# A planned order of issue for the first 14 FFN steps, batch 1's attention and the weight conversion

## The chip, the cores and the metric

The kernel runs on one core of a Trainium2 chip. The metric is the device time of one execution in microseconds (us). A core has five engines, each with its own instruction queue: TensorE (PE in the profile, PEld for its weight loads), VectorE (DVE), ScalarE (ACT), GpSimd (POOL) and SyncE (SP, which here issues the loads and stores). Engines wait for each other through semaphores. Matmuls write to eight PSUM banks of 2 KB per partition; all else lies in SBUF.

## What is computed

```python
# attention, for each of 8 batches and 8 heads (576 tokens, 64 wide)
q_d, k_d, v_d = (a.reshape(B, H, 144, 4, D).mean(axis=3) for a in (q, k, v))
out_up = np.repeat(softmax(scale * q_d @ k_d.T) @ v_d, 4, axis=2)      # coarse part
mask = np.abs(pos[:, None] - pos[None, :]) < 4
out_local = softmax(np.where(mask, scale * q @ k.T, -1e9)) @ v         # band part
x = (out_up + out_local) as 4608 tokens x 512
# FFN, 512 -> 2048 -> 512
h = x @ w_in
g = s * np.maximum(h, 0.0) ** 2 + b
return g @ w_out
```

The weights arrive as float64 and are read as pairs of 32-bit words.

## The kernel before

**FFN.** The 4608 tokens are 18 tiles of 256 (index t), the 2048 hidden columns 8 parts of 256 (index p). A step is a pair (t, p). `gemm1` (lines 551 to 570) makes one part of h in one PSUM bank: 24 matmuls over 256 columns, three for each product, since x and the weights are split into a high and a low float32r part (hi times hi, hi times lo, lo times hi; lines 556 to 558). ScalarE then applies ReLU and the square and rounds to `gh`, VectorE makes the rest `gl` (lines 566 to 569). `gemm2` (lines 586 to 616) multiplies by w_out with 12 matmuls over 512 columns and accumulates over p in two banks. It runs two steps behind `gemm1`. The order of steps (lines 653 to 656) is: 14 steps with p from 0 to 6 and t = 0, 1 in turn; t = 2 with p from 0 to 6 (steps 14 to 20); p = 7 for t = 0, 1, 2; then t from 3 on with all p. TensorE therefore meets each new part of the weights as it is converted.

**Conversion.** `convert` (lines 214 to 234) turns a staged block of float64 words into the high and low float32r parts: a scaled copy on ScalarE (line 226), four operations on VectorE (227 to 230), a rounding copy on ScalarE (231), and a subtraction on VectorE (234). `split_w(p)` does this for w_in's and w_out's part p. The scratch is a pair of tiles `pv` for p = 0, 1, 7 and the tiles `xl2` and `os` for the others. `CHUNK` sets the columns per operation, `CONVERT_AT` the step after which each part is converted, `BEHIND` how far its priority is lowered.

**Attention.** A unit is one batch and two heads. `down` (lines 268 to 342) is the coarse part: sums of four tokens on VectorE and GpSimd, scores `sa`, softmax, transposes `tp` and `tr`, and the product `up`. `first_unit` (lines 344 to 440) runs `down` for a unit of batches 0 to 2 and, between its stages, the band part with small matmuls: two score tiles `sl`, softmax, a transpose to blocks `bd`, two products `ol`. `up` is copied to `ups` (line 421), and line 434 adds `ol` and the repeated `ups` into x. Batches 3 to 7 use `two_pairs`, which does the band part on GpSimd and VectorE (`local_unit`) and the coarse part with `down_unit`, whose ScalarE copy (line 448) writes the repeated `up` into x.

Each unit takes eight PSUM tiles one after the other: sa, sl, sl, tp, tr, up, ol, ol. Batch 0 takes them from a ring of seven banks (line 638), batch 1 from banks 5 and 6 in turn, batch 2 from bank 5 and then from 2, 3 and 5 (line 662). FFN uses bank 4, bank 7 for t = 1 in the first 14 steps, and banks 0 to 3 for its sums. A bank is taken again once its last reader is done.

Batch 0's units 1 to 3 borrow tiles of the FFN (`make_room`, lines 89 to 102): the places of converted weights, and for the exponentials `pl` of units 2 and 3 parts of the tiles `os` and `xl2` (line 97).

**Order.** A scheduler in the framework fixes each engine's order of instructions when the kernel is built, by priorities and its own estimate of times; on the chip each engine follows that order. The program steers it by the order of the calls and by `high_priority(offset)`. Batch 0 has an offset of 400 (line 643). From step 0 on, `advance` (lines 680 to 686) runs the attention of later batches as a generator, so many yields per step that batch b is ready when its tokens are due (`need`, `free`, `NY`, lines 629, 658 to 678); batch 1's yields have an offset of 300. Lines 691 to 707 are the loop over steps.

`split_x(t)` (lines 529 to 546) splits a token tile into its high and low parts; tile 2 needs tokens of batches 0 and 1 and uses the tiles `os` and `xl2`. `add_rows` (lines 572 to 579) sums rows of w_out for the bias term, one part p per step, from step 13 on.

Of the kernel before, what the change touches and what calls it, by code (L numbers as in the profile page):

```python
# [11 lines left out]
F32 = mybir.dt.float32  # L12
# [50 lines left out]
def attention_ffn_kernel(ctx, tc, qk, vw_in, vr_in, vdm, qkn, vn, w_in, w_out, s_in, b_in, out):  # L63
# [127 lines left out]

    wi, wo, wst = {}, {}, {}
# [4 lines left out]
    def load_w(p):  # L197

        parts = (("i", src_i[:, :, 512 * p : 512 * p + 512]), ("o", src_o[:, 2 * p : 2 * p + 2]))
        for op, src in parts:  # L200
# [13 lines left out]
    def convert(st, hi, lo, op, p):  # L214


        n = hi.shape[1]
        top, low = st[:, :, 1], st[:, :, 0]
        if p in (0, 1, 7):
            f = two.tile([P, n], F32, tag="pv", name="es")  # L220
        else:
            f = one.tile([P, n], F32, tag="xl2" if op == "i" else "os", name="es")
        w = f.bitcast(I32)


        nc.scalar.mul(f, top.bitcast(F32), 2.0 ** -112)
        nc.vector.tensor_scalar(f, f, W_MAX, -W_MAX, ALU.min, ALU.max)
        nc.vector.tensor_scalar(w, w, 3, 0x7FFFFFF8, ALU.logical_shift_left, ALU.bitwise_and)
        nc.vector.scalar_tensor_tensor(w, low, 29, w, ALU.logical_shift_right, ALU.bitwise_or)
        nc.vector.scalar_tensor_tensor(w, top, -0x80000000, w, ALU.bitwise_and, ALU.bitwise_or)  # L230
        nc.scalar.copy(hi, f)
        for i in range(0, n, 512):
            js = slice(i, min(i + 512, n))
            nc.vector.tensor_tensor(lo[:, js], f[:, js], hi.bitcast(F32)[:, js], ALU.subtract)

    def split_w(p):
        with tc.high_priority(offset=-BEHIND.get(p, 0)):
            split_parts(p)

    def split_parts(p):  # L240
        wi[p] = one.tile([P, 2, NK, 256], F32R, tag=f"wi{p}", name="wi")
        wo[p] = one.tile([P, 2, 2, DM], F32R, tag=f"wo{p}", name="wo")
        for op, w in (("i", wi[p]), ("o", wo[p])):
            fl = w.rearrange("p s k f -> p s (k f)")
            if p < len(STAGE):
                st = wst.pop((p, op))
                for j in range(0, 1024, CHUNK[p]):
                    js = slice(j, j + CHUNK[p])
                    convert(st[:, js], fl[:, 0, js], fl[:, 1, js], op, p)
            else:  # L250
                for i in range(4):
                    cs = slice(256 * i, 256 * i + 256)
                    convert(load_quarter(p, op, i), fl[:, 0, cs], fl[:, 1, cs], op, p)
# [14 lines left out]
    def down(b, hp, banks, tmp, dg):  # L268
# [6 lines left out]
        kd = tmp([P, SD], "kd")  # L275
        nc.vector.tensor_reduce(
            qd, qt[:, 0:S].rearrange("p (s j) -> p s j", j=FAC), AX.X, ALU.add)
        nc.vector.tensor_reduce(
            kd, kt[:, 3 : 3 + S].rearrange("p (s j) -> p s j", j=FAC), AX.X, ALU.add)
        for h in range(2):  # L280
# [18 lines left out]
        dsm = tmp([P, NQ], "dsm")[0:n]  # L299
        sa = banks([n, NQ, SD], "sa")  # L300
        with first(b):
            for i in range(NQ):
                nc.tensor.matmul(sa[:, i], qc[:, i], kd, start=True, stop=True)  # L303
        nc.vector.tensor_reduce(dmx[:, 0], sa, AX.X, ALU.max, negate=True)
# [465 lines left out]
```

## Time and profile before

| | |
|---|---|
| time, median of 3 runs | 974.49 us (971.71 to 974.57) |
| the profiled execution's own time | 972.49 us |
| its span, first to last instruction | 970.7 us |
| PE busy | 938.7 us, 97% of the span |
| DVE, ACT, POOL busy | 637.7, 475.0, 418.0 us |
| mean granted TensorE clock | 1.00 |

The page gives the busy time of each engine, its share in 40 equal slices, the chain of waits that ended last, the costliest groups of instructions and the DMA issues. A row of a group reads: line, engine, operation, output <- inputs, partitions x elements, count | busy us, mean ns of one | idle time of the engine just before them and what ended it. A row of the timeline reads: start, duration, engine, line, and in brackets the idle time before it and its releaser. Matmuls are pipelined, so their durations overlap; the distance between two starts is the pace. The tiles that batch 0's units 1 to 3 borrow are all named `flat`.

### The profile page before, as it was taken

To read this page: it belongs to the slowest core of one execution; us is meant where nothing else is said; L and a number is where in the kernel's file an instruction comes from. 1 tells how busy PE (TensorE), PEld (TensorE's weight loads), DVE (VectorE), ACT (ScalarE), POOL (GpSimd) and SP (SyncE) were. 2 spreads that over 40 slices of the span, in tenths; PEclk is the share of its full clock that TensorE was granted. 3 is DMA by queue.
4 is the path that set the end of the run, shared out by engine and by line. 5 is a ranking of instruction groups with operands and counts; after the bars stand their busy time and mean duration, and the time that the engine had idled before them with its cause. 6 is when DMAs were issued, how large, how long until landed. Compare 5 with 4: busy or idle time off the path is not lost.

```text
span 970.7 us, 18541 instructions
## 1 busy us (share of the span) xinstructions
PE 938.7 (97%) x7316; PEld 843.4 (87%) x7316; DVE 637.7 (66%) x1175; ACT 475.0 (49%) x1141; POOL 418.0 (43%) x455
## 2 busy tenths in 40 slices
PE   5769999999999999999999999999999999999998
PEld 4559988888999999998888899989899999998987
DVE  5999996864567878787787878787878521211121
ACT  5878775553754453545363545453635433333231
POOL 9421011101066686776868786867676200000000
PEclk9999999999999999999999999999999999999999
DMA  9736512112243232323241424242412000000000
GB/s 316 261 121 210 172 60 78 49 42 73 101 134 113 77 110 72 102 70 133 67 136 66 135 68 131 72 134 69 136 55 76 1 22 1 23 1 22 1 23 22
DMA packets 32103, 86.26 MB, mean 89 GB/s; under 512 B 3344, under 2 KB 7952, under 8 KB 32016
## 3 DMA queue, kind: packets, MB, share of 16 engines
q1 hardware_dynamic: 32016, 85.08, 26.6%
q8 instruction: 57, 0.93, 0.4%
q14 instruction: 30, 0.25, 0.1%
HBM read 75.63 MB, written 9.44 MB: 88 GB/s over the span
## 4 chain that ended last, share of the span: by engine, by line
PE 74%; DVE 9%; DMA 8%; POOL 5%; ACT 2%; issue 2%; SPq 0%; DVEq 0%; ACTq 0%; POOLq 0%
PE ph L556 11%; PE ph L557 11%; PE ph L558 11%; PE po L603 11%; PE po L601 11%; PE po L602 11%; DMA tqk<-in_qk_dram 3%; POOL pr L466 3%; POOL acc L488 3%; DMA wst<-in_moe_w_out_dram 2%; PE sa L303 2%; DVE bias L579 1%; PE up L339 1%; PE ol L431 1%; DMA lqk<-in_qkn_dram 1%
## 5 line engine op out<-in xcount | busy, mean ns | idle before, releaser
L556 PE MATMUL ph<-xh,wi 128*128 128x256 f32 x1152 | 325.4, 283 | 3.7 <-ACT xh L542 2.5
L557 PE MATMUL ph<-xl,wi 128*128 128x256 f32 x1152 | 323.9, 281 | 0.0
L558 PE MATMUL ph<-xh,wi 128*128 128x256 f32 x1152 | 323.6, 281 | 0.0
L466 POOL TENSOR_TENSOR pr<-lqk 128x576 f32<-128x576 f32 x140 | 201.2, 1461 | 73.2 <-DMA lqk<-in_qkn_dram 29.2
L556 PEld LDWEIGHTS ph<-xh,wi 128*128 128x128 f32 x1152 | 217.5, 189 | 11.2 <-ACT xh L542 2.8
L557 PEld LDWEIGHTS ph<-xl,wi 128*128 128x128 f32 x1152 | 217.4, 189 | 5.4 <-issue 0.2
L558 PEld LDWEIGHTS ph<-xh,wi 128*128 128x128 f32 x1152 | 217.6, 189 | 0.3
L566 ACT ACTIVATE ph<-ph 128x512 f32<-128x512 f32 x144 | 83.8, 582 | 229.0 <-PE ph L558 223.2
L601 PE MATMUL po<-wo,gh 128*128 128x512 f32 x456 | 180.7, 396 | 0.0
L602 PE MATMUL po<-wo,gh 128*128 128x512 f32 x456 | 180.5, 396 | 0.0
L603 PE MATMUL po<-wo,gl 128*128 128x512 f32 x456 | 177.9, 397 | 0.0
L569 DVE TENSOR_TENSOR gl<-ph,gh 128x512 fp32r<-128x512 f32 x114 | 77.8, 683 | 115.8 <-ACT gh L568 115.5
L488 POOL TENSOR_TENSOR acc<-acc,pv 128x576 f32<-128x576 f32 x80 | 114.4, 1430 | 57.1 <-DVE acc L488 29.5
L468 DVE TENSOR_REDUCE st<-pr 128x9 f32<-128x576 f32 x140 | 105.9, 757 | 37.7 <-POOL pr L466 35.4
L292 POOL TENSOR_TENSOR dq<-vq 64x64 f32<-64x64 f32 x58 | 22.8, 393 | 197.4 <-PE up L337 195.3
L603 PEld LDWEIGHTS po<-wo,gl 128*128 128x128 f32 x456 | 85.7, 188 | 17.6 <-issue 0.2
L487 DVE TENSOR_TENSOR pv<-lv,st 128x576 f32<-128x576 f32 x120 | 87.5, 747 | 18.8 <-POOL acc L488 18.4
L601 PEld LDWEIGHTS po<-wo,gh 128*128 128x128 f32 x456 | 85.7, 188 | 15.9 <-ACT gh L568 0.6
L602 PEld LDWEIGHTS po<-wo,gh 128*128 128x128 f32 x456 | 85.7, 188 | 15.8
L568 ACT CAST gh<-ph 128x512 fp32r<-128x512 f32 x114 | 66.9, 587 | 64.3 <-PE po L602 62.4
L567 ACT ACTIVATE ph<-ph 128x512 f32<-128x512 f32 x144 | 83.7, 582 | 3.2
L602 PE MATMUL po<-wo,gb 128*128 128x512 f32 x120 | 47.1, 392 | 0.0
(149 smaller groups left out, 1239.3 us busy)
## 6 DMA issues: line engine op xcount, KB each, us to landing
tqk<-in_qk_dram SPq DMA_DIRECT2D x30, 584.0 KB, 4.1
lqk<-in_qkn_dram SPq DMA_DIRECT2D x20, 768.0 KB, 4.2
lv<-in_vn_dram SPq DMA_DIRECT2D x20, 480.0 KB, 3.4
out_dram<-os SPq DMA_DIRECT2D x17, 512.0 KB, 3.1
wst<-in_moe_w_in_dram SPq DMA_DIRECT2D x7, 1024.0 KB, 6.5
wst<-in_moe_w_out_dram SPq DMA_DIRECT2D x7, 1024.0 KB, 5.3
tvd<-in_vdm_dram SPq DMA_DIRECT2D x29, 160.0 KB, 2.9
tvr<-in_vr_dram SPq DMA_DIRECT2D x29, 128.0 KB, 3.1
```

Source lines behind the costliest of these rows:

```text
L466: nc.gpsimd.tensor_tensor(pr, lqk[:, 0:CH], lqk[:, CH + o : 2 * CH + o], ALU.mult)
L468: nc.vector.tensor_reduce(ls[:, :, o], pr, AX.X, ALU.add)
L487: nc.vector.tensor_tensor(pv, lv[:, o : o + CH], w, ALU.mult)
L488: (nc.vector if o % 3 == 1 else nc.gpsimd).tensor_tensor(acc[:, :, h], acc[:, :, h], pv, ALU.add)
L556: nc.tensor.matmul(ph[:, j], wi[p][:, 0, k, f], xh[:, k], start=(k == 0), stop=False)
L557: nc.tensor.matmul(ph[:, j], wi[p][:, 0, k, f], xl[:, k], start=False, stop=False)
L558: nc.tensor.matmul(ph[:, j], wi[p][:, 1, k, f], xh[:, k], start=False, stop=(k == NK - 1))
L566: nc.scalar.activation(ph, ph, AF.Relu)
L567: nc.scalar.activation(ph, ph, AF.Square)
L601: nc.tensor.matmul(po[m], gh[:, j, ms], wo[p][:, 0, j], start=first, stop=False)
L602: nc.tensor.matmul(po[m], gh[:, j, ms], wo[p][:, 1, j], start=False, stop=False)
L603: nc.tensor.matmul(po[m], gl[:, j, ms], wo[p][:, 0, j], start=False, stop=last)
```

## The change

1. The functions of attention, conversion, `split_x`, `gemm1` and `gemm2` become generators. Before each piece of work they yield a record of it: engine, estimated us, whether it takes or gives back a PSUM bank, and a condition.
2. `plan()` runs the first 14 FFN steps, batch 1's four units and the conversion of p = 1 to 6 as parallel streams through a small simulation with these estimates, and issues each piece when the simulation begins it. Among pieces that could begin on an engine within `WAIT` of the first, the lowest rank goes first. All of this stands in `tc.manual_schedule(engines=ENGINES)`: TensorE, VectorE and ScalarE follow the order of issue there. SyncE and GpSimd don't stand in that set.
3. The conversion in the plan has four lanes, each with a scratch of 512 columns in `xl2` or `os`, for p = 1 too. For w_out of p = 1 to 6 the subtraction on VectorE becomes a negated copy on ScalarE and a DMA issued from GpSimd that adds f to it. For a p = 7 chunk, and for p = 0, the work is as before.
4. `first_unit` is parted into `down_unit` and `band_unit`. `up` is copied by ScalarE, repeated, into x (as in `down_unit` before), and the band part adds `ol` to x; `ups` goes. Within the plan, `tr` is taken after `tp` is copied.
5. Batch 0 takes its banks from two couples of four, 0 to 3 for even and 4 to 7 for odd units; the two parts of a unit follow each other in the order AABBBAABABB, which is the order that `first_unit` had.
6. In batch 2 the coarse part of the next unit runs between the stages of the band part of this one.
7. Behind the plan, split_x(2) and the conversion of p = 7 follow; before, they came with step 13 and step 11. `add_rows` starts one step later. `NY` counts 11 yields per unit.

```diff
-CONVERT_AT = (1, 2, 4, 6, 7, 8, 11)
-CHUNK = (512, 512, 512, 1024, 1024, 512, 1024)
-BEHIND = {1: 400, 2: 100, 4: 100, 5: 400}
+CHUNK = 512
+ADDED, X_AT, LOAD, LAT, BUSY, LANES, WAIT = 5.0, 12.0, 9.0, 0.2, 1.7, 4, 0.25
+PACE, PAIR = 6.6, 22.0
+TURNS = "AABBBAABABB"
+BY_TRANSFER = [(op, p) for op in "o" for p in range(1, 7)]
...
+        yield step("A", 0.62)
+        nc.scalar.mul(f, top.bitcast(F32), 2.0 ** -112)
+        yield step("V", 0.36)
+        nc.vector.tensor_scalar(f, f, W_MAX, -W_MAX, ALU.min, ALU.max)
...
+        if adds:
+            yield step("A", 0.62)
+            nc.scalar.mul(lo, f, -1.0)
+            nc.gpsimd.dma_start(lo, f, accum_op=ALU.add)
+            yield step("D", ADDED)
         else:
-            f = one.tile([P, n], F32, tag="xl2" if op == "i" else "os", name="es")
...
+            yield step("V", 0.64)
+            nc.vector.tensor_tensor(lo, f, hi.bitcast(F32), ALU.subtract)
...
+    def down_unit(b, hp, banks):
+        x = new_x(b)
+        up = yield from down(b, hp, banks, spot(b, hp), diag[0 if b else hp])
+        yield step("A", 0.66, give=True)
+        nc.scalar.copy(
+            x[:, hp].rearrange("p (s j) -> p s j", j=FAC),
+            up.unsqueeze(2).to_broadcast([P, SD, FAC]))
+        yield
...
-            nc.vector.tensor_tensor(
-                x[:, hp, f * (S // 2) : (f + 1) * (S // 2)].rearrange("p (s j) -> p s j", j=FAC),
-                ol.rearrange("p (s j) -> p s j", j=FAC),
-                ups[:, n * f : n * f + n].unsqueeze(2).to_broadcast([P, n, FAC]), ALU.add)
+            yield step("V", 0.45, give=True)
+            xf = x[:, hp, f * (S // 2) : (f + 1) * (S // 2)]
+            nc.vector.tensor_tensor(xf, ol, xf, ALU.add)
...
+    def plan():
+        free = {"P": 0.0, "A": 0.0, "V": 0.0, "D": 0.0}
+        held = {5: 0.0, 6: 0.0}
+        streams = []
+        todo = [(p, op, i) for p in range(1, HF) for op in "io" for i in range(1024 // CHUNK)]
...
+                slow = 1.0 if at > X_AT or engine == "P" else BUSY
+                self.ready = at + us * slow + LAT
+                if engine != "D":
+                    free[engine] = at + us * slow
...
+                down_stream[0].rank = X_AT + PAIR * (hp + 1) - 8.0
+                yield from down_unit(1, hp, lambda *a: down_stream[0].bank(*a))
...
+                band_stream[0].rank = X_AT + PAIR * (hp + 1)
+                yield from band_unit(1, hp, lambda *a: band_stream[0].bank(*a))
...
+                me[0].rank = X_AT + PACE * (2 * p + 2 * (op == "o")) - 6.0
+                yield from split_chunk(p, op, i, f)
...
+        while streams:
+            begins = [(s.begin(), s) for s in streams]
+            begins = [(at, s) for at, s in begins if at is not None]
+            at, s = min(begins, key=lambda b: b[0])
+            engine = s.want[0]
+            at, s = min(((a, s) for a, s in begins if s.want[0] == engine and a <= at + WAIT),
+                        key=lambda b: (b[1].rank, b[0]))
+            s.emit(at)
...
-    bk = banks(0, 1, 2, 3, 5, 6, 7)
+    couples = banks(0, 1, 2, 3), banks(4, 5, 6, 7)
...
-            for _ in first_unit(0, hp, bk):
+            bk = couples[hp % 2]
+            for _ in in_turn("AABBBAABABB", A=coarse(down_unit(0, hp, bk)), B=coarse(band_unit(0, hp, bk))):
...
+    with tc.manual_schedule(engines=ENGINES):
+        plan()
+    done = NY[1]
+    for _ in split_x(2):
+        pass
+    split_w(NFP - 1)
     for st, (t, p) in enumerate(order):
-        gemm1(t, p)
...
+        if st < 2 * HF:
+            continue
```

The FFN stream has the rank infinity, so it yields to the others where both could begin; the evictions have the rank -1 and come first. X_AT is the time on the plan's own clock at which x of batch 0 is expected; operations of ScalarE and VectorE that begin earlier are taken to last BUSY times as long. Loads of weights for p + 2 are issued when a part's last chunk is done, loads of batch 1's units from the coarse stream.

More of the change, by code (lines that the diff above doesn't have):

```diff
@@ L189, in clear, with step, run, coarse @@
         diag[i] = (take(da, 0, [P, 2 * NG, P]), *blocks(da, n, vm))
+    def step(engine, us, take=False, give=False, when=None):
+        return engine, us, take, give, when
+    def run(gn):
+        for _ in gn:
+            pass
+    def coarse(gn):
+        for said in gn:
+            if said is None:
+                yield
     wi, wo, wst = {}, {}, {}
@@ L212, in load_quarter, with convert @@
         return st
[L214 to L217 removed]
+    def convert(st, hi, lo, f, adds=False):
         top, low = st[:, :, 1], st[:, :, 0]
[L219 to L234 removed]
@@ L236, in split_w @@
-    def split_w(p):
[L237 to L253, printed above, removed]
+        w = f.bitcast(I32)
@@ L513, in two_pairs @@
             load_pair(b, 2 * g + u)
-        dn = chain(*(down_unit(b, 2 * g + u, banks) for u in range(2)))
+        dn = chain(*(coarse(down_unit(b, 2 * g + u, banks)) for u in range(2)))
         lo = local_unit(b, g, banks)
```

303 lines of the change are left out of this document (239 added, 64 removed).

## The prediction

> **What bounds the kernel now.** I read the page's first part, busy time by engine, and then the same in five stretches that I cut at the first dense FFN matmul (69.24), at the first matmul of step 14 (159.25) and at step 28 (250.50).
>
> ```profile
> PE 938.7 (97%) x7316; PEld 843.4 (87%) x7316; DVE 637.7 (66%) x1175; ACT 475.0 (49%) x1141; POOL 418.0 (43%) x455
> ```
>
> ```profile
> core 0: us, PE busy (x) PEld busy (x) DVE busy (x) ACT busy (x) POOL busy (x), PEclk, DMA share, GB/s
> 0.00:25.00 25.00, 14.16 (x281) 11.22 (x281) 13.01 (x29) 12.15 (x39) 22.68 (x64) 1.00 0.96 315
> 25.00:69.24 44.24, 30.67 (x421) 25.01 (x421) 43.01 (x98) 36.44 (x96) 15.10 (x18) 1.00 0.56 189
> 69.24:159.25 90.01, 90.01 (x902) 80.76 (x900) 81.73 (x156) 66.57 (x143) 10.66 (x18) 1.00 0.43 142
> 159.25:250.50 91.25, 89.49 (x861) 77.25 (x860) 59.04 (x113) 44.34 (x110) 7.67 (x12) 1.00 0.19 62
> 250.50:970.70 720.20, 714.37 (x4857) 649.15 (x4855) 440.91 (x782) 315.52 (x755) 361.88 (x344) 1.00 0.22 72
> ```
>
> From 69.24 on TensorE is busy in 90.01 of 90.01, 89.49 of 91.25 and 714.37 of 720.20 us: 7.6 us of idle time in 901. It is the bound there, and the change takes no matmul away, so nothing is to be had in that part. The head is another matter: 69.24 us pass before the dense matmuls, TensorE idles 10.84 + 13.57 = 24.4 us in them, and in the second stretch the full engine is VectorE, 43.01 of 44.24. So I ask two things: how much earlier the first step can start, and how much longer the 14 steps then take. What is left of the difference runs through to the end.
>
> The TensorE rows around the first step show how its queue behaves.
>
> ```profile
> 64.57 0.58 PE L556 MATMUL ph<-xh,wi 128*128 128x256 f32 x1 [2.50 <-ACT xh L542]
> 67.06 2.24 PE L431 MATMUL ol<-db,tvw 128*64 128x96 f32 x24 [1.91 <-ACT db L414]
> 69.24 0.58 PE L557 MATMUL ph<-xl,wi 128*128 128x256 f32 x1
> ...
> 69.83 0.41 PE L556 MATMUL ph<-xh,wi 128*128 128x256 f32 x1
> 70.04 0.41 PE L557 MATMUL ph<-xl,wi 128*128 128x256 f32 x1
> ...
> 73.07 0.28 PE L558 MATMUL ph<-xh,wi 128*128 128x256 f32 x1
> 73.19 0.28 PE L556 MATMUL ph<-xh,wi 128*128 128x256 f32 x1
> ```
>
> Step 0 begins at 64.57 with one matmul. Its second stands behind 24 matmuls of batch 1's first unit (db, tvw), which idle 1.91 us for a copy of ScalarE. So issue order alone cost 2 to 4 us. The pitch falls from 0.21 to 0.12 us between 70 and 73: the first 3 us run at half pace, a cost that the change moves and doesn't remove.
>
> The VectorE rows of batch 0: the maximum of the coarse scores of units 0, 1 and 3, the last sum into x of units 1 (44.46) and 3 (65.35), and the first split of x.
>
> ```profile
> 9.04 0.60 DVE L304 TENSOR_REDUCE dmx<-sa 96x3 f32<-96x432 f32 x1 [1.91 <-PE sa L303]
> ...
> 18.56 0.59 DVE L304 TENSOR_REDUCE flat<-sa 96x3 f32<-96x432 f32 x1
> ...
> 34.17 0.59 DVE L304 TENSOR_REDUCE flat<-sa 96x3 f32<-96x432 f32 x1
> ...
> 44.46 0.45 DVE L434 TENSOR_TENSOR x<-ol,flat 128x288 f32<-128x288 f32 x1
> ...
> 65.35 0.44 DVE L434 TENSOR_TENSOR x<-ol,flat 128x288 f32<-128x288 f32 x1
> 65.72 1.21 DVE L543 TENSOR_TENSOR xl<-x,xh 128x1024 fp32r<-128x1024 f32 x1
> ```
>
> From unit 0 to unit 3 the maxima lie (34.17 - 9.04)/3 = 8.4 us apart. Unit 1 needs 26.4 us from its maximum to x, unit 3 even 31.6.
>
> **Part 1: the head.** Two things change in it.
>
> First, the banks. In the ring of seven, unit 1's second local score tile stands on the bank of unit 0's transposed weights, its next ones on unit 0's up and ol, and so on along the chain. With couples, units 0 and 1 share no bank; unit 2 waits only for unit 0, unit 3 only for unit 1.
>
> Second, what VectorE does beside it. These groups are from the stretch 25.00 to 69.24.
>
> ```profile
> L229 DVE SCALAR_TENSOR_TENSOR es<-wst,es 128x512 int32<-128x512 int32 x10 | 6.8, 675 | 0.0
> L230 DVE SCALAR_TENSOR_TENSOR es<-wst,es 128x512 int32<-128x512 int32 x10 | 6.6, 675 | 0.0
> L227 DVE TENSOR_SCALAR es<-es 128x512 f32<-128x512 f32 x10 | 4.8, 493 | 0.4 <-ACT es L226 0.4
> L228 DVE TENSOR_SCALAR es<-es 128x512 int32<-128x512 int32 x10 | 4.4, 440 | 0.0
> ...
> L234 DVE TENSOR_TENSOR wo<-es,wo 128x512 fp32r<-128x512 f32 x4 | 2.7, 668 | 0.0
> ```
>
> Ten chunks of 512 columns go through: four of p=0, which steps 0 and 1 want, and six of p=1 and 2, which they don't. A chunk costs (6.8 + 6.6 + 4.8 + 4.4)/10 + 0.67 = 2.93 us. The six are 17.6 us of the 43.01. In the changed kernel they can't stand there: their scratch is now xl2 and os, which hold the exponentials of batch 0's units 2 and 3 (make_room, line 97) until those are transposed; before, p=1 used pv, which was free. So about 43.0 - 17.6 = 25.4 us of VectorE work remains (with some of batch 1's first unit in it), and by VectorE alone step 0 could start at 25 + 25.4 = 50. By the chain: two units at a time, each in unit 1's 26.4 us, which is with today's crowding. Units 0 and 1 go from 10 to 36; unit 3's scores start when unit 1 has given back their bank, somewhere halfway, at 23, and end at 49; the split of x, 1.2 us, gives 50 too. As in-order waits come on top, I take 55. The ends are 49 (everything fits) and 65 (only the 4 us of issue order go).
>
> **Part 2: the 14 steps.** They now hold all four units of batch 1, and so one more than the 90.01 us did, (1,0). Its price comes from the pitch:
>
> ```profile
> 104.06 0.39 PE L601 MATMUL po<-wo,gh 128*128 128x512 f32 x1
> 104.29 0.39 PE L602 MATMUL po<-wo,gh 128*128 128x512 f32 x1
> ...
> L557 PE MATMUL ph<-xl,wi 128*128 128x256 f32 x112 | 32.5, 290 | 0.0
> ...
> L602 PE MATMUL po<-wo,gh 128*128 128x512 f32 x48 | 19.3, 402 | 0.0
> ```
>
> In the stretch stand 3 x 112 matmuls at 0.12 and 3 x 48 at 0.23 us, 40 + 33 = 73 us, plus 1.5 for the slow start. The remaining 15.5 us are three units: 5.2 each. Dense, the 14 steps take 90.0 + 5.2 = 95.2.
>
> Do the others keep up? VectorE did 13.0 + 43.0 + 81.7 = 137.7 us up to step 14. Off it go 12 subtractions of 0.67 (8 us) and the quarters of p=7 that now follow the plan (up to 10, from five of the 256-wide chunks). So about 120 to 130 us stand against 55 + 95 = 150, less the 12 us that VectorE idles in the first 25. It fits, at 90%. ScalarE did 12.2 + 36.4 + 66.6 = 115.2. On it come 12 negated copies and the wider copies of up, 8 of them up to step 14:
>
> ```profile
> L448 ACT COPY x<-up 128x576 f32<-128x576 f32 x20 | 12.8, 642 | 11.0 <-PE up L339 10.7
> ```
>
> That is at most 8 x 0.64 = 5 us, and 12 x 0.64 = 8 us by the same row: 128 us. Both engines have room, but with three engines at 85 to 100%, each issuing in a fixed order, waits like the 1.91 us above will occur. Thirty-two bank takes of batch 1 and 14 evictions stand in the order; I take 3 us in all, from none to 12. So the 14 steps take 98.
>
> **The adds by transfer.** No row shows one. The nearest is a 256 KB load:
>
> ```profile
> wst<-in_moe_w_in_dram SPq DMA_DIRECT2D x4, 256.0 KB, 2.8
> ```
>
> An add reads two streams and writes one, so 2.8 to 5.6 us; the planner allows 5.0, and wo of p is wanted two steps after wi, 11 us. I take no cost. If one lands later than planned, ScalarE's next chunk on that scratch waits and the evictions stand behind it; 0.6 us x 12 = 7 us is the dear end. The other end is below nothing, since a lane freed before plan only helps. The two single-source operations L227 and L228 are the place to look for trouble: together 0.93 us per chunk, so an issue on GpSimd that had to wait one pair out would come to 3.7, still inside 5.0. The Trainium skill, page "SBUF — State Buffer", section "SBUF: two separate sides", speaks against this edit: a transfer issued from GpSimd starves for descriptors while VectorE runs such an operation, and one of about 620 ns took about 3100. By its added 2.5 us a transfer would take 5.3 and cost 12 x 0.3 = 4 us at most; no run so far shows it.
>
> GpSimd's queue holds batch 1's sums over v behind these issues; it is busy 10.66 of 90.01 us, which covers them. SyncE's loads are the same ones, at 0.43 of the DMA engines. Batch 2's new order uses the same banks, in a stretch where VectorE is 65% busy: nothing. Step 14 needs all of batch 1 for split_x(2), which now comes behind the whole plan: 0 to 3 us, I take 0.5.
>
> **Sum.** 55 + 98 + 0.5 + (91.25 + 720.20) = 965, and 1.8 around the span (the execution took 972.49 for a span of 970.7): 967. The profiled execution lies 2.0 below the median of 974.49. About 0.3%, 2.9 us, is what can be told from no change: faster is below 971.6, slower above 977.4.
>
> **Rivals.** *The head stays long*: the last unit is held by GpSimd and the loads, as the first stretch's 22.68 of 25 us and DMA share of 0.96 suggest, and only issue order is gained: 65 + 98 + 812 + 2 = 977. Against it: from 25 on both are half idle. *The fixed order stalls* (the other sign): batch 1's pieces stand in TensorE's queue at estimated times, and every estimate that is short holds the FFN behind it, as at 64.57. Twelve to fifteen us more in the 14 steps: 979 to 982. It decides once waits exceed 69.24 - 55 - 5.2 = 9 us, five like the 1.91 seen. For it: TensorE then has no idle time to hide them. Against it: the estimates follow the rows (0.64 for L229's 0.675). *The adds starve*, ScalarE's queue with them: 4 to 7 us, about 973, later still if they are beyond 6 us each. *All fits*: 49 + 95.2 + 811.5 + 1.8 = 957.5.
>
> **Chances.** The forecast 0.50, the long head 0.15, the stalls 0.17, the starved adds 0.04, all fits 0.14. Faster: 0.44 + 0.02 + 0.02 + 0 + 0.14 = 0.62. Same: 0.06 + 0.07 + 0.04 + 0.01 = 0.18. Slower: 0 + 0.06 + 0.11 + 0.03 = 0.20. The forecast's own range is 958 to 973; to leave out no more than 2 in 10, I reach to 956 and 979.
>
> **What would show it.** The first dense matmul of FFN near 55, not 65; the maxima of units 0 and 1 within 4 us; no chunk of p=1 before unit 2's transpose; step 14 at about 153; TensorE's idle time over 3 us in the 14 steps if the order stalls, with releasers among batch 1's lines; adds at 3 to 5 us from issue to landing. If step 14 comes no earlier than 159, I am wrong, and the split between its two terms says where.

## The result: slower

The changed kernel takes 1003.44 us (median of 4, 1001.39 to 1005.37), the kernel before 973.3 beside it: a ratio of 1.032, interval 1.0303 to 1.0338. I had said 967. The profiled execution took 1001.39 us for a span of 999.6. First the page's engine row, then the stretches, cut at the same matmuls as before: the first of the FFN (58.34), the first of step 14 (170.16), and the one at which I had cut at 250.50 (271.43; it is the first of step 27 when steps are counted from 0).

```profile
PE 950.5 (95%) x7316; PEld 849.6 (85%) x7316; DVE 645.9 (65%) x1187; ACT 487.4 (49%) x1165; POOL 431.2 (43%) x467
```

```profile
core 0: us, PE busy (x) PEld busy (x) DVE busy (x) ACT busy (x) POOL busy (x), PEclk, DMA share, GB/s
0.00:25.00 25.00, 12.99 (x232) 10.61 (x232) 14.29 (x30) 12.65 (x41) 22.68 (x64) 1.00 0.95 304
25.00:58.34 33.34, 21.35 (x384) 17.91 (x384) 29.68 (x69) 28.39 (x69) 9.27 (x12) 0.71 0.63 213
58.34:170.16 111.82, 104.36 (x1017) 90.93 (x1016) 95.95 (x198) 85.42 (x194) 21.95 (x36) 0.96 0.55 154
170.16:271.43 101.27, 91.69 (x856) 77.27 (x854) 60.69 (x115) 48.45 (x124) 8.73 (x18) 0.98 0.21 67
271.43:999.60 728.17, 720.08 (x4835) 652.85 (x4833) 445.31 (x779) 312.44 (x739) 368.55 (x338) 1.00 0.21 70
```

Against before, the head is 69.24 - 58.34 = 10.9 us shorter, the 14 steps 21.8 longer, the next stretch 10.0, the tail 8.0: 28.9 in all, the difference of the spans. Two things stand out. TensorE executes as many matmuls as before (7316), yet is busy for 950.5 us instead of 938.7; in the tail it does 22 fewer and needs 720.08 instead of 714.37. And between 170 and 271, where it had idled 1.8 us, it idles 9.6. (The 14 steps hold two `gemm2` more than before, 24 x 0.234 = 5.6 us that are missing later.)

The head's time came as forecast. These are VectorE's maxima of units 0 to 3, and TensorE's first FFN matmuls:

```profile
9.06 0.60 DVE L341 TENSOR_REDUCE dmx<-sa 96x3 f32<-96x432 f32 x1 [1.91 <-PE sa L339]
...
15.21 0.59 DVE L341 TENSOR_REDUCE flat<-sa 96x3 f32<-96x432 f32 x1
...
26.22 0.59 DVE L341 TENSOR_REDUCE flat<-sa 96x3 f32<-96x432 f32 x1
...
29.25 0.56 DVE L341 TENSOR_REDUCE flat<-sa 96x3 f32<-96x432 f32 x1
```

```profile
56.96 1.75 PE L339 MATMUL sa<-kd,dq 128*96 128x144 f32 x6 [3.40 <-ACT dq L317]
58.34 0.59 PE L634 MATMUL ph<-xh,wi 128*128 128x256 f32 x1
58.73 0.41 PE L635 MATMUL ph<-xl,wi 128*128 128x256 f32 x1
```

Units 2 and 3 now start 3 us apart, each with its couple. In front of the first step stands a score of batch 1, though, for which TensorE waits 3.40 us, and the first 4.5 us of FFN run at half pace (clock 0.5 until 62.8 us), as some 3 us did before (there the spacing of 0.21 us shows it, although the view gives a clock of 1.00).

Up to step 12 the planned order was kept: for the steps 1 to 12 the planner's clock and the trace lie 46.4 to 48.0 us apart. Then it slipped. Step 13 came 2.2 us later than at step 12's distance, behind a wait of 2.21 us for `pd` at 154.11, and batch 1's last sum into x, at 116.5 on the planner's clock, came at 168.7, some 5 us late. Five quarter chunks of slice 7, which the plan doesn't hold, ran before step 14. Of the 6 to 13 us by which the steps 0 to 6 were early, step 12 had nothing left (0.7 us late), and step 14 was 10.9 late.

### The profile page after: what moved, and what is told of

Its sections match the earlier page's. It is cut to its first block, busy times and chain, and to the rows that moved or that the text cites. A ratio compares the mean times of both kernels' runs of the same rounds, so it can differ in the third digit from the quotient of the medians.

```text
span 999.6 us, 18611 instructions
## 1 busy us (share of the span) xinstructions
PE 950.5 (95%) x7316; PEld 849.6 (85%) x7316; DVE 645.9 (65%) x1187; ACT 487.4 (49%) x1165; POOL 431.2 (43%) x467
## 4 chain that ended last, share of the span: by engine, by line
PE 58%; DVE 15%; DMA 10%; POOL 8%; issue 4%; ACT 3%; SPq 0%; DVEq 0%; POOLq 0%; ACTq 0%
PE ph L634 9%; PE ph L636 9%; PE ph L635 9%; PE po L690 9%; PE po L691 9%; PE po L692 9%; POOL pr L539 5%; DMA tqk<-in_qk_dram 3%; DMA lqk<-in_qkn_dram 3%; POOL acc L561 2%; DVE pv L560 2%; DMA wst<-in_moe_w_out_dram 1%; DVE gl L657 1%; DVE st L541 1%; DVE es L250 1%
## 5 line engine op out<-in xcount | busy, mean ns | idle before, releaser
L634 PE MATMUL ph<-xh,wi 128*128 128x256 f32 x1152 | 329.6, 286 | 6.0 <-DVE gl L657 4.2
L636 PE MATMUL ph<-xh,wi 128*128 128x256 f32 x1152 | 326.3, 283 | 0.0
L539 POOL TENSOR_TENSOR pr<-lqk 128x576 f32<-128x576 f32 x140 | 209.7, 1524 | 105.9 <-DMA lqk<-in_qkn_dram 77.2
```

The source lines that it names most:

```text
L539: nc.gpsimd.tensor_tensor(pr, lqk[:, 0:CH], lqk[:, CH + o : 2 * CH + o], ALU.mult)
L634: nc.tensor.matmul(ph[:, j], wi[p][:, 0, k, f], xh[:, k], start=(k == 0), stop=False)
L636: nc.tensor.matmul(ph[:, j], wi[p][:, 1, k, f], xh[:, k], start=False, stop=(k == NK - 1))
```

## The experiments

18 kernels were run, each beside the kernel before. Times are medians; ratios are to the kernel before.

| run | base and edit | us | ratio, interval |
|---|---|---|---|
| e1 | changed, addresses of before | 993.62 | 1.0223 (1.0202 to 1.0244) |
| e4 | before, addresses of changed | 980.48 | 1.0082 (1.0067 to 1.0096) |
| e6 | changed, batch 2 in the old order | 993.77 | 1.0226 (1.0206 to 1.0247) |
| e8 | changed, both (the base below) | 986.65 | 1.0157 (1.0138 to 1.0177) |
| e16 | base, no adding transfers | 977.25 | 1.0052 (1.0034 to 1.007) |
| e17 | base, ScalarE's copies without transfers | 988.15 | 1.0149 (1.0133 to 1.0165) |
| e3 | before, couples alone | 980.42 | 1.0084 (1.0071 to 1.0098) |
| e13 | e3, slice 7 and bias late | 976.75 | 1.0045 (1.0027 to 1.0062) |
| e12 | base, slice 7 and bias late | 981.21 | 1.0087 (1.0068 to 1.0106) |
| e9, e10, e11 | base, e3, before: slice 7 late | 1000.27, 985.01, 984.28 | 1.0292, 1.0134, 1.0125 |
| e15 | base, units due every 12 us | 983.73 | 1.0116 (1.0096 to 1.0136) |
| e22 | e16, units due every 18 us | 984.28 | 1.014 (1.0117 to 1.0163) |
| e18 | e12 without transfers | 983.51 | 1.0095 (1.0076 to 1.0114) |
| e19 | e18, units due every 14 us | 979.05 | 1.0058 (1.0041 to 1.0076) |
| e20 | changed, x moved by 32 bytes | 1001.37 | 1.0285 (1.0261 to 1.031) |
| e21 | changed, all moved by 64 bytes | 1001.82 | 1.0311 (1.0284 to 1.0337) |

### Addresses: e1, e4, e20, e21

The tile `ups` (576 bytes per partition) goes, and every tile that is allocated behind it moves down. By the allocation of the two kernels, x's halves lay at offset 32 modulo 128 bytes and lie at 96 now; the w_in halves of p = 2 to 6 lay and lie at 96, those of p = 0, 1, 7 went from 96 to 32.

```diff
# e1: changed kernel                               # e4: kernel before
+    one.tile([P, SD], F32, tag="ups", name="ups") | -return one.tile(shape, F32, tag=name, name=name)
     split_w(0)                                    | +return one.tile(shape, F32, tag="ptr" if name == "ups" else name, name=name)
```

> The changed kernel with one unused tile of 576 bytes per partition put back where the removed tile ups was, so that x, the halves of the weights and every later tile lie at the addresses that they had before the change; no instruction is different. Theory 1 (places): in the changed kernel the rows of x and those of five of the eight weight slices have the same offset modulo 128 bytes, and the matmuls that read both start 118.8 to 119.3 ns apart instead of 114.6 to 116.7; with the old places the spacing goes back to about 115 in the slices 2 to 6 and the time falls by 24 matmuls x 3.7 ns x some 85 steps = 7.5 us, with the second matmuls' share up to 10: 993 to 997 us. Theory 2 (order only): the spacing comes from what runs beside the matmuls, stays at 119, and the time stays at 1002 to 1004.

> The kernel before with one edit: the tile ups shares the place of ptr, so that it no longer takes 576 bytes of its own and every later tile lies where it lies in the changed kernel; the order of all instructions is that of before. Theory 1 (places): the spacing of the first matmuls in the slices 2 to 6 rises from 115 to 119 ns, and the time by 7 to 10 us, to 980 to 984. Theory 2 (order only): 972 to 975, the spacing as before.

One step near the end, p = 3 of the last tile, with no attention beside it: its first matmul and the first of the `gemm2` behind its 24. In this order: before, changed, e1, e4.

```profile
932.86 0.28 PE L556 MATMUL ph<-xh,wi 128*128 128x256 f32 x1
...
935.59 0.39 PE L601 MATMUL po<-wo,gh 128*128 128x512 f32 x1
```

```profile
960.94 0.28 PE L634 MATMUL ph<-xh,wi 128*128 128x256 f32 x1
...
963.79 0.39 PE L690 MATMUL po<-wo,gh 128*128 128x512 f32 x1
```

```profile
956.54 0.28 PE L634 MATMUL ph<-xh,wi 128*128 128x256 f32 x1
...
959.27 0.39 PE L690 MATMUL po<-wo,gh 128*128 128x512 f32 x1
```

```profile
937.83 0.28 PE L556 MATMUL ph<-xh,wi 128*128 128x256 f32 x1
...
940.68 0.39 PE L601 MATMUL po<-wo,gh 128*128 128x512 f32 x1
```

24 matmuls take 2.73, 2.85, 2.73 and 2.85 us: 113.8 or 118.8 ns each, and it goes with the addresses, not with the order. In e4 the order of instructions on every engine is that of the kernel before, and the tail of 4857 matmuls (714.37 of 720.20 us before) becomes this:

```profile
249.92:976.20 726.28, 721.94 (x4857) 656.15 (x4855) 444.81 (x782) 315.89 (x755) 365.16 (x344) 1.00 0.22 71
```

So 7.6 us of TensorE time in e4's tail, 8.7 us in its median, and 9.8 us back in e1. Theory 1 held in both directions, with one difference: slice 6, whose weights lie 64 bytes from x too, was not among the fast ones. The median spacing over the last tiles went from 113.5 to 114.3 ns before to 118.7 to 120.0 in e4 for the slices 2 to 5, and from 117.4 to 120.0 for slice 6.

```diff
# e20, behind most tiles: the split x, g and the weights of p = 1 move by 32 bytes
+    one.tile([P, 8], F32, tag="pad", name="pad")
     order = [(t, p) for p in range(HF) for t in range(2)]
# e21: the same line with [P, 16], ahead of x, g and all weights
```

> The changed kernel with an unused tile of 32 bytes per partition that moves x, g and slice 7's weights alone, by 32 bytes: x then lies at offset 0 modulo 128, the weights of the slices 2 to 6 still at 96, those of slices 0 and 1 at 32, of 7 at 64. Theory 1 (the same offset of x and weights is what slows a pair of reads): the spacing in the slices 2 to 6 goes from 119.0 to 114 to 116 ns, as with the old places (x at 32), and the time to 992 to 997. Theory 2 (x at 32 was fast by itself, or the difference has to be 64): the spacing stays at 119 and the time at 1001 to 1005.

> The changed kernel with an unused tile of 64 bytes per partition ahead of all tiles of x, g and the weights: x goes from offset 96 to 32 modulo 128 (the offset that was fast), the weights of the slices 2 to 6 from 96 to 32, the others from 32 to 96; every difference between two tiles is that of the changed kernel. Theory 1 (only the difference counts): the spacing in the slices 2 to 6 stays at 118 to 120 ns and the time at 1000 to 1005. Theory 2 (x at 32 is fast by itself): spacing 114 to 117, time 992 to 997.

The same step in e21 and in e20:

```profile
959.75 0.28 PE L636 MATMUL ph<-xh,wi 128*128 128x256 f32 x1
...
962.60 0.39 PE L692 MATMUL po<-wo,gh 128*128 128x512 f32 x1
```

```profile
960.86 0.28 PE L634 MATMUL ph<-xh,wi 128*128 128x256 f32 x1
...
963.68 0.41 PE L690 MATMUL po<-wo,gh 128*128 128x512 f32 x1
```

2.85 us where all tiles moved together: x at 32 is not fast by itself, the distance between the two operands counts. With x at 0 it is 2.82. By the allocation it was slice 1's weights that moved along with x in e20, not slice 7's as I had expected: slice 1 stays 64 bytes from x and at 117.8 ns, while the slices 0 and 7, now 32 from it, slow down from 117.7 to 119.7. So "the same offset is slow, another is fast" fell. In every slice that was seen at more than one distance, 64 bytes modulo 128 was the fastest: 113.5 to 114.3 ns in the slices 2 to 5, against 117.4 to 118.7 at 32 and 118.3 to 120.0 at 0. Why 64 gains only 2 ns in the slices 0, 6 and 7 stays open.

### Batch 2's order: e6, e8

```diff
-            load_ahead(HP * b)
-            yield from batch(b, rings[b])
+            for hp in range(HP):
+                load_ahead(HP * b + hp)
+                ring = rings[b](hp)[1]
+                yield from in_turn(
+                    TURNS, A=coarse(down_unit(b, hp, ring)), B=coarse(band_unit(b, hp, ring)))
```

> The changed kernel with batch 2's attention in the order of before: the two halves of one unit interleaved, one bank for units 0 and 1 and three for 2 and 3, instead of the second half of a unit interleaved with the first half of the next. Theory 1 (batch 2's new order is part of the loss): the steps 16 to 36 lag the kernel before by 5 us less than in the changed kernel (+18 instead of +22.9 at step 36), 996 to 999 us. Theory 2 (the order of batch 2 is a matter of nothing, the lag in these steps comes from the attention that lies in them whatever its order): 1002 to 1004. Should slice 7's conversion or the adds of x wait longer in the old order, it would be slower than 1004.

The stretch from step 14 on takes 92.7 us up to 265.40, in place of 101.27:

```profile
172.69:265.40 92.71, 87.58 (x837) 75.94 (x836) 57.38 (x111) 44.74 (x109) 6.58 (x12) 0.94 0.19 62
```

9.7 us come back. In the changed kernel the coarse part of unit (2,0) is issued alone, ahead of everything; TensorE's and ScalarE's rows show what that does:

```profile
176.97 0.28 PE L373 MATMUL tp<-ident,pd 96*80 96x96 f32 x1 [3.27 <-ACT pd L356]
...
178.36 0.44 PE L370 MATMUL tr<-ident,pd 96*64 96x96 f32 x3 [0.95 <-ACT ptm L383]
```

```profile
168.84 0.84 ACT L617 CAST xh<-x 128x768 fp32r<-128x768 f32 x1
171.81 0.43 ACT L244 ACTIVATE es<-wst 128x256 f32<-128x256 f32 x1 [2.13 <-DMA wst<-in_moe_w_out_dram]
172.15 0.62 ACT L317 COPY dq<-qd 64x144 f32<-64x144 f32 x2
...
175.91 1.00 ACT L356 ACTIVATE pd<-pd,dsm 96x144 f32<-96x144 f32 x3
```

The unit's transposes stand in TensorE's queue in front of FFN matmuls and idle it 3.27 us for `pd`. On ScalarE a 256-column chunk of slice 7 stands in front of the unit and waits 2.13 us for its load; how much of the 3.27 it makes isn't separated. From 170 to 285 TensorE's waits by the wait view are 3.3 us for that `tp`, 1.7 for `tr`, 1.7 for the output's evacuation and 1.6 for `gl`; in e6 the longest is 2.0.

> The changed kernel with both of the edits that gained 10 us each: the old addresses (an unused tile of 576 bytes) and batch 2 in the old order. Theory 1 (two causes that don't touch each other): 1003.4 - 9.8 - 9.7 = 984, 982 to 986 us, with the spacing of before and the steps from 36 on lagging the kernel before by no more than 12 to 14 us, all of which is there at step 16 already. Theory 2 (one cause seen twice): 990 to 994.

986.65: 16.8 of the 19.5 us. Mostly two causes, with 2.7 us in common.

### The adding transfers: e16, e17

```diff
-BY_TRANSFER = [(op, p) for op in "o" for p in range(1, 7)]
+BY_TRANSFER = []                                         # e16
...
             nc.scalar.mul(lo, f, -1.0)                   # e17
-            nc.gpsimd.dma_start(lo, f, accum_op=ALU.add)
-            yield step("D", ADDED)
+            yield step("V", 0.64)
+            nc.vector.tensor_tensor(lo, f, hi.bitcast(F32), ALU.subtract)
```

> The base (986.65 us) with no adding transfers: the second halves of the twelve w_out chunks of slices 1 to 6 are made by a subtraction on VectorE, as those of w_in are. VectorE gets 12 x 0.69 = 8.3 us more between 60 and 150, ScalarE 12 x 0.62 = 7.4 us less and GpSimd 12 us of issue less. Theory 1 (VectorE's time bounds the steps up to 14, the reason for which I had given the adds a gain): step 14 later by 5 to 8 us, 991 to 995. Theory 2 (it doesn't: TensorE waits for the chain of batch 1 through three engines, and by the planner's clock the last FFN piece moves by under 2 us): 984 to 989.

> The base (changed kernel, old addresses, batch 2 in the old order; 986.65 us) with ScalarE's twelve negated copies kept, but the halves then made by VectorE's subtraction instead of the adding transfer. So it has the ScalarE load of the base (12 x 0.62 = 7.4 us more than the run without transfers) and the VectorE load of the run without transfers (977.25 us). Theory 1 (the loss comes with ScalarE's copies, in whose queue batch 1's and batch 2's exponentials stand): 983 to 988 us. Theory 2 (it comes with the transfers: their issue behind GpSimd's other work, their landing, the temporary tile that they hold): 976 to 980.

Without transfers it is 9.4 us faster, which neither theory had; with ScalarE's copies kept and VectorE's subtraction in the transfers' place it is as slow as the base. So going back from the transfers to the subtraction gains nothing as long as the copies stay. In the changed kernel the transfers' row of the DMA issues reads

```profile
wo<-es POOLq DMA_DIRECT2D x12, 256.0 KB, 4.7
```

A median of 4.7 us, within the planner's 5.0; the shortest took 3.3, the longest 8.2, and ScalarE waited for one of them once, 1.4 us. In this order the 9.4 us come with the twelve copies on ScalarE. (In e17 the subtraction must also wait for the copy, whose place it overwrites; that isn't separated.) The 14 steps and the next stretch, e16 with its tail, then e17, then the base:

```profile
58.02:167.73 109.71, 101.52 (x1018) 87.90 (x1016) 102.06 (x209) 78.67 (x181) 12.60 (x24) 0.98 0.40 131
167.73:253.34 85.61, 83.70 (x833) 73.30 (x832) 57.73 (x111) 44.69 (x109) 6.42 (x12) 0.98 0.20 66
253.34:974.60 721.26, 715.85 (x4857) 649.94 (x4855) 443.70 (x782) 316.59 (x755) 362.87 (x344) 1.00 0.22 72
```

```profile
60.18:173.22 113.04, 103.44 (x1017) 90.12 (x1016) 102.11 (x210) 85.93 (x194) 12.45 (x24) 0.97 0.40 129
173.22:265.08 91.86, 87.17 (x833) 75.87 (x832) 57.12 (x110) 44.00 (x108) 6.56 (x12) 0.94 0.18 59
```

```profile
59.37:170.08 110.71, 100.88 (x1018) 87.45 (x1016) 96.41 (x198) 84.93 (x194) 22.21 (x36) 0.99 0.55 156
170.08:262.06 91.98, 85.91 (x834) 74.51 (x833) 57.37 (x111) 44.26 (x108) 6.79 (x12) 0.96 0.19 63
```

ScalarE has 7.3 us more to do in e17's 14 steps than in e16's, and they are 3.3 longer; in the base they are 1.0 longer. The larger part, 6.3 and 6.4 us, lies in the next stretch, where ScalarE's work is the same. There TensorE executes as many matmuls (832 and 833); in e17 it idles 2.8 us more than in e16 and is busy 3.5 us longer, at a mean granted clock of 0.94 instead of 0.98. What differs between the two is the order that the framework's scheduler gives behind the plan. In e17, as in the changed kernel, a chunk of ScalarE waits for its load between x's third block and unit (2,0); in e16 none does:

```profile
170.74 0.84 ACT L617 CAST xh<-x 128x768 fp32r<-128x768 f32 x1 [0.69 <-DVE x L500]
173.48 0.44 ACT L244 ACTIVATE es<-wst 128x256 f32<-128x256 f32 x1 [1.91 <-DMA wst<-in_moe_w_out_dram]
173.82 0.61 ACT L317 COPY dq<-qd 64x144 f32<-64x144 f32 x2
```

```profile
165.11 0.82 ACT L617 CAST xh<-x 128x768 fp32r<-128x768 f32 x1
167.75 0.41 ACT L254 CAST wo<-es 128x256 fp32r<-128x256 f32 x1 [1.82 <-DVE es L252]
168.06 0.63 ACT L317 COPY dq<-qd 64x144 f32<-64x144 f32 x2
```

But in e16 a chunk that waits 1.82 us for VectorE stands in the same place, and unit (2,0) follows x's third block after 2.95 us there and after 3.08 in e17. So this row alone doesn't explain the difference. How much of the 9.4 us is ScalarE's load and how much the reordering isn't separated.

### The couples, and where the head's gain went: e3, e13

> The kernel before with one part of the change alone: batch 0's units take their banks from two rings of four in turn, instead of one ring of seven. Theory 1 (the head's gain is real and comes from this part): the last x add of batch 0 comes 6 to 9 us earlier, near 57, the first dense matmul at 58 to 60 instead of 69, and the time falls by 4 to 8 us, 965 to 969. Theory 2 (the gain needs the conversion's new order as well, since slice 0's conversion and batch 1's first unit then fill the same engines): the end of batch 0 moves by under 3 us and the time is 971 to 974.

Both theories missed: the head gained (first FFN matmul at 57.58, step 13 at 141.16 instead of 151.94), and the kernel lost 8.7 us. Step 14 came at 170.64 instead of 159.25. It needs batch 1's last sum into x; here is that row before and, in a fence of its own, the group of VectorE's quarter chunks of slice 7 between 60 us and that row, and then the same two for e3:

```profile
155.41 0.45 DVE L434 TENSOR_TENSOR x<-ol,ups 128x288 f32<-128x288 f32 x1
```

```profile
L230 DVE SCALAR_TENSOR_TENSOR es<-wst,es 128x256 int32<-128x256 int32 x4 | 1.7, 419 | 0.1
```

```profile
170.24 0.45 DVE L434 TENSOR_TENSOR x<-ol,ups 128x288 f32<-128x288 f32 x1
```

```profile
L230 DVE SCALAR_TENSOR_TENSOR es<-wst,es 128x256 int32<-128x256 int32 x7 | 2.9, 410 | 0.1
```

Four chunks stood in front of it, now seven; they come 5 to 7 us apart, each loaded only when the one before has freed its place. But batch 1 is late from its start. Before, the last sums of its four units begin at 71.7 (in time that TensorE had free), 103.2, 130.4 and 155.4 us; in e3 they begin at 87.6, 119.5, 149.9 and 170.2. The lag of 16 us is there at the first two units, before the chunks of slice 7 come (from 138 us on, but for one). So the chunks can't have made it; at most they keep it from being made up. To test that I queued them, on ScalarE, behind x's third block:

```diff
+            mark[t] = nc.scalar.copy(xh[:, :, dst], src)
...
+            with tc.issue_after(getattr(mark[2], "ins", mark[2])):
+                split_w(NFP - 1)
```

They come from step 15 on, and `add_rows` takes the parts in the order 0 to 7.

> The same kernel (old addresses, batch 2 in the old order) with slice 7's eight quarter chunks queued on ScalarE behind the copy of x's third block, so that they run in the steps 14 to 20 and no longer between batch 1's pieces; the bias rows are added slice 0 first, since slice 7 comes last. Theory 1 (the quarters, which are loaded one by one through one staging tile, stand in front of batch 1's last unit in the queues of ScalarE and VectorE and hold it): the last x add of batch 1 moves from 170 to 158 to 163, step 14 from 172 to 160 to 165, the lag at step 16 falls by 6 to 10 us; what is left of it at the end depends on step 21, which needs slice 7: if the chain of eight quarters of 6 us each ends by 215, 974 to 979 us, if it is late there by some us, 980 to 984. Theory 2 (batch 1's own chain sets step 14): its last x add stays at 168 to 171 and the time at 983 to 986 or above.

> The kernel before with batch 0's banks by couples and slice 7's conversion behind the copy of x's third block. Theory 1 (the couples' gain of 7 us in the head is lost because the quarters of slice 7 stand in front of batch 1's last unit): step 14, at 170.6 with the couples alone and at 159.3 before, comes at 150 to 158, and the time is 964 to 970, under the kernel before. Theory 2 (VectorE's work up to step 14 is what counts, or batch 1's first unit, which the couples moved behind the first FFN steps): step 14 stays at 165 to 171 and the time is 977 to 982.

> The kernel before with slice 7's conversion behind the copy of x's third block, nothing else. Theory 1: VectorE has four of the eight quarters fewer in front of step 14, 4 x 2.5 = 10 us of busy time; step 14 moves from 159.3 to 150 to 156, the time is 966 to 971 if step 21 doesn't wait, else 972 to 976. Theory 2: step 14 is set by the dense work in front of it (14 steps of 6.44), stays at 157 to 160, and the time is 971 to 974.

All three were slower than their bases, by 13.6, 4.6 and 12.6 us: with slice 7 last, the additions to the bias (31 x 0.68 = 21 us of VectorE) came forward into the gap, in e9 with waits for the adding transfers. So these runs don't answer the question. With the bias held back too:

> The kernel before with the couples, slice 7's conversion and the additions to the bias behind the copy and the subtraction of x's third block. With the couples alone it took 980.42 us, the last x add of batch 1 at 170.2 and step 14 at 170.6 (before: 155.4 and 159.3). Theory 1 (seven quarters of slice 7 stood in front of that add, four before): last x add at 145 to 156, step 14 at 150 to 158, the time 966 to 974. Theory 2 (with the couples the FFN's earlier start puts the conversions of slices 1 to 6 and the evictions ahead of batch 1, whatever slice 7 does): last x add at 162 to 172 and the time 976 to 984.

> The run with slice 7 late, repeated with the 31 additions of the weight rows into the bias queued on VectorE behind the subtraction of x's third block too (in that run they had come forward into the gap that slice 7's chunks left). Base: the changed kernel with old addresses and batch 2 in the old order, 986.65 us, batch 1's last x add at 168.6, step 14 at 170.1. Theory 1 (work that nobody needs before step 21 stands in the queues of VectorE and ScalarE in front of batch 1's last unit): last x add at 158 to 163, step 14 at 160 to 165; VectorE then has 21 + 22 us of it in the 45 us of steps 14 to 20, so that step 21 may wait: 978 to 986 us in all, with the lag at step 14 smaller by 5 to 10 us in any case. Theory 2 (the planned order itself sets the end of batch 1): last x add at 167 to 170, step 14 at 169 to 171.

e13 gained 3.7 us on e3 (last sum into x at 162.3), e12 5.4 on the base (163.2 instead of 168.6). The first lies in the second theory's ranges, the second in or near the first theory's. So work that is wanted only from step 21 on does stand in the way, but moving it returns some 40% of the loss: VectorE then has it between steps 14 and 21. Batch 1's late first unit wasn't tested by itself. VectorE's busy time from 40 us to step 21, in the kernel before and in e13:

```profile
40.00:213.90 173.90, 161.59 (x1626) 141.43 (x1625) 152.62 (x301) 116.29 (x266) 22.54 (x32) 1.00 0.33 108
```

```profile
40.00:218.10 178.10, 163.97 (x1642) 141.70 (x1642) 150.94 (x300) 118.39 (x271) 21.04 (x38) 0.92 0.33 106
```

The same 151 to 153 us of VectorE in a stretch that got no shorter, although the FFN's first matmul came at 56.7 instead of 64.57.

### The planner's due times: e15, e22, e18, e19

> The base (changed kernel, old addresses, batch 2 in the old order; 986.65 us) with batch 1's units due every 12 us instead of every 22 in the planner (PAIR). By the planner's own clock the last piece of batch 1 then starts at 85 instead of 116.5 and the last FFN piece at 111.9 instead of 111.8; the chip has kept that clock to within 2 us. Theory 1 (step 14 waits for the planner's order, which puts batch 1's last unit behind the 14th step): last x add at 132 to 142, step 14 at 160 to 164 instead of 170.1, and the time 977 to 981. Theory 2 (the conversions that are put off come late on the chip, through the adds on GpSimd's queue or slice 7's chunks): step 14 at 168 to 172, 984 to 989.

> The run without adding transfers (977.25 us; addresses and batch 2's order of before) with batch 1's units due every 18 us instead of 22. In the planner's clock its last unit's last piece starts at 98.5 instead of 112.6, the last FFN piece at 113.3 instead of 113.1. Theory 1 (what is left is step 14's wait for batch 1's last unit, whose last x add came at 165.0): last x add at 146 to 153, step 14 at 161 to 165 instead of 167.7, time 972 to 975. Theory 2 (an earlier attention only pushes the conversions back, as in the two runs with due times of 12 and 14): step 14 at 166 to 169 and 976 to 981.

> The run with slice 7 and the bias late (981.21 us) without adding transfers. Theory 1 (the two gains, 5.4 and 9.4 us from the base of 986.65, add): 970 to 974, step 14 at 160 to 164. Theory 2 (both remove the same wait in front of step 14 and in the steps 14 and 15): 976 to 979.

> The same with batch 1's units due every 14 us instead of 22. Theory 1 (in the planner's clock the last unit then ends 27 us earlier and the last FFN piece at 113.5, so step 14 follows the thirteenth without a wait): 3 us less than the run beside it, 967 to 971, faster than the kernel before by 1 to 4 us. Theory 2 (an earlier attention only moves the waiting from batch 1 to the conversions, as its due time of 12 us did: steps 6 to 12 were 5 to 13 us later there): the same time as beside it or up to 4 us more, 970 to 978.

e15 had the last sum into x at 137.6, 31 us earlier, and gained 2.9: steps 4 to 12 came 5 to 13 us later, as the conversions were put off. e22 had it at 146.5 and step 14 at 163.5, 4.3 us before e16's, and lost 7.0: by step 19 it was 6.2 behind, with six of slice 7's eight chunks still to come behind step 14, where e16 had three. e18 lost 6.3 on e16, so the gains don't add, and e19 came between. Against e12 (1.0087), e18 (1.0095) has neither copies nor transfers and is no faster: the 9.4 us that their removal gave in the base are not there when slice 7 and the bias come late. They are a price of the copies in one order of the queues, not of the copies as such. No due time that was tried beats 977.25, and none of the 18 kernels beats the kernel before.

## Why the prediction was wrong, step by step

- **Head, 55 taken.** 58.34, inside 49 to 65, but by one of my two reasons. VectorE was relieved less than I wrote (29.68 us instead of 25.4; six chunks of 512 columns ran there, not four, and one of slice 7). And e3, with the couples but the conversion of before, starts the FFN at 57.58 with 29.99 us of VectorE work from 25 us on: the couples give the gain, the new scratch isn't needed for it. The maxima of units 0 and 1 lay 6.1 us apart, not 4.
- **14 steps, 98.** 111.82, or 106.2 without the two `gemm2` that moved in. The failed step is "Both engines have room". The sum was wrong: VectorE did 14.3 + 29.7 + 96.0 = 139.9 us up to step 14, not 120 to 130. Five quarters of slice 7 ran before step 14, as before the change, and the 28 chunks of 512 columns take 65.0 us in their first four operations, where 16 of 512 and 6 of 1024 took 60.0. And the comparison was wrong: I set sums of busy time against the stretch, while batch 1's end is reached through a chain in three queues, in which slice 7's chunks and the copies stand too. By the planner's own clock the FFN starts at 12.8 and batch 1's last sum at 116.5, so the plan itself is longer than 98. ScalarE's copies I costed as 8 us within its room; taking them away gave 9.4 us in the base, and nothing with slice 7 late.
- **Waits of 3 us in the 14 steps.** TensorE idles 7.5 us there, most of it for `pd` and `pl` of batch 1. That is the sign that the stalling rival named, and 106.2 is near its size; but its mechanism, estimates that are short, shows only at the end of the plan, from step 13 on. The half pace of 4.5 us at the start and of 3.4 us from 155.0 on (clock 0.50) costs some 4 us more, of which I had 1.5.
- **"Batch 2's new order uses the same banks ...: nothing."** A term that I put at nothing: 9.7 us when undone alone, 7.0 when undone after the addresses. I looked at VectorE's load and not at what the unit's transposes hold up in TensorE's queue.
- **The rest taken over unchanged, 91.25 + 720.20 = 811.45.** 829.4, or 835.0 with the two `gemm2` that left it. I had no step at all for a removed tile moving the others: 9 us in either direction. In a kernel that is bound by dense matmuls, 4 to 5% of the pace of `gemm1` in four slices of eight and 2% in a fifth are worth nearly as much as the head's 10.9 us.
- **Step 14 "at about 153".** 170.16, and by my own line ("no earlier than 159") that was the sign. The head's 10.9 us were gone there already: of my two terms it is the second that failed.
- **Adds "at 3 to 5 us".** 4.7 at the median, right, though single ones took up to 8.2. The rule from the Trainium skill's page "SBUF — State Buffer", section "SBUF: two separate sides", is that a transfer issued from GpSimd starves for descriptors while VectorE runs a two-port operation. This trace neither shows nor excludes it: the median lies within the 2.8 to 5.6 that I had without the rule, the longest beyond it. That it cost time isn't seen: e17, which has none of the transfers, is no faster than the base.

Of the 30.1 us between the two kernels the runs undo, one after the other, 9.8 (addresses), 7.0 (batch 2) and 9.4 (copies); 977.25 against 972.43 remains, in which the head's gain is contained. In e16 everything behind step 14 takes 85.61 + 721.26 + 5.6 = 812.5 us, about as before (811.45), and the head is 11.2 us shorter. So the remainder lies in the 14 steps: 109.71 us, or 104.1 without the two `gemm2`, where before they took 90.01 and I had forecast 98. What keeps it there, and with it which order would turn the head's gain into time, stays open: slice 7's place, the bias and the due times each move it, and none of them removed it.

## What to carry to other kernels

Starting the bounding engine earlier was worth nothing here while what it waits for next came no earlier: find the last date that an input of the next stage has, and what stands in front of it in each queue. Moving that one input isn't enough either: e15 had it 31 us earlier and gained 2.9, as other work came late instead. What an edit gains in one order of the queues need not hold in another. A reordering outside a plan is part of the change: price the work that an automatic scheduler will place between. Before comparing two kernels whose tiles differ, compare the addresses of the operands of the dense loop; undoing a shift costs one unused tile.

## What the hardware showed that I had not expected

With the same instructions in the same order, 24 matmuls of 256 columns take 2.73 or 2.85 us depending on where the moving and the stationary operand lie in SBUF relative to each other. With x above byte 204,000 of the partition and w_in halves between 15,200 and 75,000 (slices 2 to 5), the median spacing was 113.5 to 114.3 ns at 64 bytes apart modulo 128, 117.4 to 118.7 at 32 and 118.3 to 120.0 at 0. For slice 6, at 95,072, it was 117.4, 118.7 and 119.6 to 120.0. For the slices from 117,000 up it was 117.7 at 64 and 119.7 at 32. Moving all tiles together changed nothing.
